# Attention and expert layer on one core: transposes gathered into longer runs, and one round of four PSUM banks

## The chip, the core and the metric

The kernel runs on one core of one Trainium2 chip. The metric is the device time of one execution in microseconds (us), the median of several runs. The engines are TensorE (PE in the profile: matmuls, and weight loads as PEld), VectorE (DVE), ScalarE (ACT), GpSimd (POOL) and SyncE (SP), which issues most of the DMAs. Every engine takes its own instructions in order; engines wait for each other through semaphores. PE writes into PSUM, which has eight banks of 128 x 512 words; DVE and ACT read them out.

## What is computed

Causal attention with a decay, and behind it a layer of eight experts of which each token takes one. Cut to what matters:

```python
# q, k, v: (8, 8, 576, 64); f: (8, 8, 576)
cum = np.cumsum(np.log(np.clip(f, 0.0001, 1.0)), axis=-1)
scores = q @ k^T / sqrt(64) + cum[..., :, None] - cum[..., None, :]
scores = where(causal mask, -1e9, scores); scores -= max over the row
attn = exp(scores); attn /= sum over the row + 1e-9
x = (attn @ v) as (4608 tokens, 512)
# experts: logits = x @ w_gate; e = argmax; gate = softmax's share of e
out = gate * (relu(x @ w1[e]) @ w2[e])
```

## The kernel before

**Pairs and steps.** The attention stage goes over 32 pairs of heads (four pairs to each of the 8 batches), numbered n. A pair's 2 x 576 rows are cut into tiles: (j, t) is head j's tile t of 128 rows, t = 0 to 3, and the last 64 rows of both heads make one joint tile. A row tile t meets only t+1 column tiles, since the mask cuts off the rest. The main loop (L732 to L815) gives each pair seven steps i = 0 to 6. Steps 0 and 1 compute the scores of (0,3) and (1,3), 512 columns each; step 2 those of (0,2) and (0,0) in one bank; step 3 (1,2) and (1,0); step 4 (0,1) and (1,1); step 5 the joint tile in two halves of 288 columns, in two banks.

**What is done with a score tile.** PE computes it (`smm`, L414) into a bank of the pool `ps_s`, which has three banks and goes round. DVE adds the mask, takes the row's extreme and writes the result to SBUF (`s_red`, L421; a short record behind it reads the accumulator). ACT takes the exponential in place (`s_exp`, L428). One pair later PE turns (transposes) the tile in blocks of 128 x 128 (`turn`, L477) into a bank, and ACT and DVE copy the bank to the array aT (`copy_on`: L473 on ACT, L471 on DVE). Step i of pair n holds the turns of pair n-1's tile of the same step: `t_steps(n - 1)[i]`. The larger tile of a bank is copied by ACT, the small ones (0,0) and (1,0) by DVE out of the same bank, and the tiles of step 4 by DVE. The joint tile's last 68 columns are turned right behind its second half, in that half's bank (`t_last`). Two pairs later, in step 1, PE multiplies with v (`av`, L553) and ACT copies out (L561).

**Between them, every fourth pair a batch is finished.** `fin_tasks` puts tasks into steps of the four pairs that follow: turning the batch's result back into rows of tokens (`fin_x`: four turns, then DVE's scaling into a row tile, L599, and a DMA to x_dram), the gate's logits (`fin_logits`), and the routing's small steps on DVE. The four pairs of such a group are told apart below as first to fourth: n = 6, 10, 14, ... are first. DVE also rounds the next pair's k (`k_first`, L373), and POOL prepares the rest of its operands.

**Order.** The engines' queues follow the order in which the loop writes the work: a step's scores and their DVE reductions, then tasks in `among`, then the step's turns with their copies, then the step's exponentials on ACT, then, in step 1, the products with v, then the step's `tasks`. Nothing is reordered afterwards (`InOrder.pin`).

**Banks.** Three for scores, two for turns (`ps_t`), one each for the two products with v and the tasks in alternation (`ps_v`, `ps_m`), and one fixed for routing.

## Time and profile before

| what | value |
|---|---|
| median of three runs (792.42 to 795.17) | 792.57 us |
| the profiled execution's own time | 791.58 us |
| its span | 789.8 us |
| PE busy, share of the span | 768.5 us, 97% |
| DVE, ACT, POOL busy | 587.0, 511.2, 543.8 us |
| granted TensorE clock, mean | 0.999 |
| DVE waits of L471 for ACT's L473 | 2.9 us in 8 waits |

The attention stage fills about the first 331 us of the span, the experts the rest. A row of the profile has the engine, the source line, the operation, what it writes and reads by the program's names, and the shape; the timeline's rows begin with the start and the duration in us, and a bracket tells what idle time came before and what ended it. `x4` is the number of instructions that a row merges.

### The profile page before, as it was taken

The numbers are of one execution on the slowest core, as the hardware profiler recorded it, in microseconds if no ns is written. First come the engines' busy times: TensorE is split into PE (matmuls) and PEld (weight loads), VectorE is DVE, ScalarE is ACT, GpSimd is POOL, SyncE is SP. The second block draws the span as 40 slices with busy tenths as digits, with TensorE's granted clock in tenths as the row PEclk, the third lists the DMA queues.
The fourth block names the chain that finished last, engine by engine and source line by source line (L and its number), as shares of the span: only waits on it lengthen the run. The fifth ranks groups of instructions, "written<-read, shape, count | busy, mean of one in ns | idle before, by whom it ended". The sixth has DMA issues, their size and how long they took to land.

```text
span 789.8 us, 16191 instructions
## 1 busy us (share of the span) xinstructions
PE 768.5 (97%) x5496; PEld 672.3 (85%) x5496; DVE 587.0 (74%) x1654; ACT 511.2 (65%) x1278; POOL 543.8 (69%) x466
## 2 busy tenths in 40 slices
PE   4999999999999999999999999999999999999996
PEld 3888888888888888888999899898898998998985
DVE  6688989898989899755589848578497487485630
ACT  6798888888888888944466546366366465463621
POOL 6999898989898989753487647556565575475311
PEclk9999999999999999999999999999999999999999
DMA  7998877787787874533445362353433433523200
GB/s 182 224 208 188 198 182 189 188 185 183 180 200 174 203 173 120 178 114 118 124 134 160 107 198 83 103 189 93 143 105 107 156 93 107 181 70 110 98 28 32
DMA packets 66825, 114.70 MB, mean 145 GB/s; under 512 B 8295, under 2 KB 39015, under 8 KB 63412
## 3 DMA queue, kind: packets, MB, share of 16 engines
q1 hardware_dynamic: 59700, 93.71, 45.8%
q0 software_dynamic: 6400, 19.93, 7.8%
q8 instruction: 44, 0.72, 0.4%
q14 instruction: 41, 0.34, 0.1%
q10 hardware_dynamic: 640, 0.01, 0.0%
HBM read 94.05 MB, written 20.55 MB: 145 GB/s over the span
## 4 chain that ended last, share of the span: by engine, by line
PE 89%; DVE 6%; ACT 2%; POOL 1%; SPq 1%; issue 1%; DMA 1%; POOLq 0%; DVEq 0%; ACTq 0%
PE ps L1200 29%; PE ps L1400 19%; PE ps L414 14%; PE ps L553 10%; PE ps L477 9%; PE ps L1170 4%; PE pr L1400 1%; DVE sc L421 1%; PE ps L1356 1%; DVE qk L373 1%; ACT sc L428 1%; DVE aT L471 1%; SPq L217 1%; ACT aT L473 1%; PE pr L993 1%
## 5 line engine op out<-in xcount | busy, mean ns | idle before, releaser
L428 ACT ACTIVATE sc<-sc,nmx 128x512 f32<-128x512 f32 (+3 forms) x256 | 142.3, 558 | 7.3 <-DVE nmx L421 5.5
L414 PE MATMUL ps<-qk 128*128 128x288 f32 (+4 forms) x384 | 124.9, 356 | 10.7 <-ACT qk L355 10.4
L421 DVE CUSTOM_DVE_ANT_0 sc<-ps,mask 128x512 f32<-128x512 f32 (+3 forms) x256 | 115.1, 483 | 16.4 <-PE ps L414 15.1
L1200 PE MATMUL ps<-w_0w,hhw 128*128 128x512 f32 x280 | 112.9, 403 | 0.0
L1400 PE MATMUL ps<-X_0w,w1s 128*128 128x320 f32 x504 | 111.7, 309 | 0.0
L1200 PE MATMUL ps<-w_0w,hl 128*128 128x512 f32 x280 | 110.8, 396 | 0.0
L1200 PE MATMUL ps<-w_1w,hhw 128*128 128x512 f32 x280 | 110.4, 394 | 0.0
L414 PE MATMUL ps<-k,q 68*128 68x288 f32 (+4 forms) x384 | 107.2, 327 | 1.5 <-DMA q<-xT0w 1.5
L1208 POOL DMA_INDIRECT out<-y,si_fast x37 | 37.3, 1009 | 96.6 <-ACT y L1207 87.6
L473 ACT COPY aT<-ps 128x512 f32<-128x512 f32 (+1 forms) x156 | 82.8, 531 | 20.4 <-PE ps L477 20.2
L553 PE MATMUL ps<-aT,va_t 128*64 128x256 f32 (+3 forms) x896 | 94.6, 354 | 0.0
L330 POOL TENSOR_TENSOR k<-raw,qk 64x1152 fp32r<-64x1152 f32 x30 | 79.8, 2659 | 18.4 <-DVE qk L373 18.4
L330 POOL TENSOR_TENSOR qk<-raw,qk 64x1280 fp32r<-64x1280 f32 x30 | 88.1, 2936 | 2.4
L1400 PEld LDWEIGHTS ps<-X_0w,w1s 128*128 128x128 f32 x504 | 84.3, 188 | 0.0
L414 PEld LDWEIGHTS ps<-qk 128*128 128x128 f32 x384 | 71.1, 197 | 14.1 <-ACT qk L355 10.4
L1207 ACT ACTIVATE y<-ps,g_fast 128x512 f32<-128x512 f32 x37 | 25.5, 690 | 87.0 <-PE ps L1200 64.9
L553 PEld LDWEIGHTS ps<-aT,va_t 128*64 128x64 f32 x896 | 58.9, 137 | 26.0 <-issue 0.7
L1400 PE MATMUL ps<-X_1w,w1s 128*128 128x320 f32 x252 | 77.9, 309 | 0.0
L414 PEld LDWEIGHTS ps<-k,q 68*128 68x128 f32 x384 | 72.7, 199 | 3.0 <-issue 2.6
L1447 POOL TENSOR_TENSOR u<-u,u 128x320 f32<-128x320 f32 x27 | 23.7, 878 | 60.6 <-DVE u L1445 60.3
L1200 PEld LDWEIGHTS ps<-w_0w,hl 128*128 128x128 f32 x280 | 52.5, 187 | 12.8
L1200 PEld LDWEIGHTS ps<-w_1w,hhw 128*128 128x128 f32 x280 | 52.8, 189 | 11.0
(242 smaller groups left out, 1900.6 us busy)
## 6 DMA issues: line engine op xcount, KB each, us to landing
raw<-in_qkT SPq DMA_DIRECT2D x52, 608.0 KB
w1r<-in_w SPq DMA_DIRECT2D x112, 128.0 KB
w<-in_w SPq DMA_DIRECT2D x28, 512.0 KB
va_t<-in_va SPq DMA_DIRECT2D x32, 256.0 KB
x_dram<-row SPq DMA_DIRECT2D x32, 256.0 KB
raw<-in_qkT SPq DMA_DIRECT2D x12, 320.0 KB
wraw<-in_w SPq DMA_DIRECT2D x7, 512.0 KB
raw<-in_qkT SPq DMA_DIRECT2D x12, 288.0 KB
```

What stands on the lines that cost most here:

```text
L330: return eng.tensor_tensor(o, raws[n][p0 : p0 + 64, c0:c1], ops[n][0][p0 : p0 + 64, c0:c1].bitcast(F32), ALU.subtract,)
L414: note(nc.tensor.matmul(out, ql[:, q0 : q0 + P], kl[:, j, k0 : k0 + kw], start=(i == 0), stop=(i == last),))
L421: V.tensor_tensor_reduce(dst[:, 0 : src.shape[1]], src, m, -0.125, init, ALU.add, ALU.min, nms[n][:, col : col + 1],)
L428: nc.scalar.activation(x, x, AF.Exp, bias=nms[n][:, col : col + 1], scale=-1.0, accum_out=acc)
L473: nc.scalar.copy(dst, src)
L477: note(nc.tensor.transpose(out.bitcast(F32R), words, c.identr))
L553: c.last_av = note(nc.tensor.matmul(pv[j * HD : (j + 1) * HD, q0 - qa : qb - qa], l, r, start=(blk == 0), stop=(blk == nb - 1),))
L1170: c.note(nc.tensor.matmul(ph[:, 0:n], w[:, wi, fs], x[xi][:, kt, :], start=(k == 0), stop=(k == 3 * KT - 1),))
L1200: c.note(nc.tensor.matmul(py, rows(hi_, ft), w[wi], start=(ft + k == 0), stop=(ft == FT - 1 and k == 2),))
L1207: nc.scalar.activation(y, py, AF.Copy, scale=g[:, s : s + 1])
L1208: nc.gpsimd.indirect_dma_start(out=self.out, out_offset=bass.IndirectOffsetOnAxis(ap=si[:, s : s + 1], axis=0), in_=y, in_offset=None, bou ...
L1400: self.nc.tensor.matmul(bank[:, 0:HN], w[:, wi, mat, kt], x[xi][:, kt, :], start=start and k == 0, stop=k == 5, skip_group_check=True,)
```

## The change

Three things. The first turns of a pair, those of tile (0,3), move from step 0 of the next pair to the end of step 5 of their own, behind the last turns of the pair before. The turns of the third and fourth tiles, (0,2) with (0,0) and (1,2) with (1,0), stand together in step 3. And the turns, the products with v, the row tasks and the logits all take their bank from one round of four (`ps_t`, `ps_t`, `ps_v`, `ps_m`). Some tasks move by a step or to the front of a step's turns (`~1` means among, ahead of the turns of step 1).

```diff
         def t_tiles(n, items, engs):
             aT = aTs[n]
-            pt = psum(ps_t)
+            pt = next_bank()
...
+        banks = itertools.cycle((ps_t, ps_t, ps_v, ps_m))
+        next_bank = lambda: psum(next(banks))
         lasts = {}
...
-            for (qa, qb, nb), bank in zip(AV, (ps_v, ps_m)):
-                pv = psum(bank)
+            for qa, qb, nb in AV:
+                pv = next_bank()
...
-            r = [(0, 3, lg[0]), (1, 0, lambda: fin_logits(b, 1, ps_m)), (1, 1, softmax),
-                 (1, 1, expert), (2, 1, gate)]
+            r = [(0, 4, lg[0]), (1, ~1, lg[1]), (1, 1, softmax), (1, 1, expert), (2, 1, gate)]
...
-                r += [(0, 2, fx[0]), (0, 4, fx[1]), (2, 2, fx[2]), (2, 3, fx[3]), (3, 1, slot),
+                r += [(0, 3, fx[0]), (0, 5, fx[1]), (2, 3, fx[2]), (2, 4, fx[3]), (3, 1, slot),
                       (3 + late, 1, lo), (3, 2, hi), (4, late, table)]
-                r += [(4, 0, lambda: fin_x(b, 4, bank=ps_m)) if late else (3, 3, fx[4])]
+                r += [(4, ~1, fx[4]) if late else (3, 3, fx[4])]
...
+        turns = {1: (1,), 3: (2, 3), 4: (4,), 5: (5,)}
...
             ts_ = t_steps(n - 1) if 0 < n <= NP else []
+            if ts_:
+                ts_[0] = None
...
-                if ts_ and ts_[i]:
-                    step(ts_[i])
+                for k in (turns if n < NP else {i: (i,)}).get(i, ()) if ts_ else ():
+                    if ts_[k]:
+                        step(ts_[k])
+                if i == 5 and n < NP:
+                    step(t_steps(n)[0])
```

What this does to the queues, in pair n = 12, a third of its group. On ACT, before, from the copy of the turns of (0,2) to the copy of the joint turns (`aT_97` is the array of the pair before, `sc_02_59` the scores of (0,2)):

```order
L473 COPY aT_97<-ps 128x3x128
L428 ACTIVATE sc_02_59,ssum<-sc_02_59,nmx 128x384
L428 ACTIVATE sc_02_59,ssum<-sc_02_59,nmx 128x128
L473 COPY aT_97<-ps 128x3x128
L428 ACTIVATE sc_12_65,ssum<-sc_12_65,nmx 128x384
L428 ACTIVATE sc_12_65,ssum<-sc_12_65,nmx 128x128
```

and now:

```order
L429 ACTIVATE sc_02_59,ssum<-sc_02_59,nmx 128x384
L429 ACTIVATE sc_02_59,ssum<-sc_02_59,nmx 128x128
L474 COPY aT_97<-ps 128x3x128 x2
L429 ACTIVATE sc_12_65,ssum<-sc_12_65,nmx 128x384
L429 ACTIVATE sc_12_65,ssum<-sc_12_65,nmx 128x128
```

The first copy has moved behind the two exponentials of (0,2) and (0,0). On DVE, in the same pair, before, from the reduction of (0,0) to that of (1,1) (`128x128` copies are the small tiles, L599 the rows of a finished batch):

```order
L421 ISA sc_02_59,nmx<-ps,mask 128x128
L421 ISA nmx 128x1
L471 COPY aT_97<-ps 128x128
L599 TENSOR_TENSOR row<-ps,rinv 128x512
L421 ISA sc_12_65,nmx<-ps,mask 128x384
L421 ISA nmx 128x1
L421 ISA sc_12_65,nmx<-ps,mask 128x128
L421 ISA nmx 128x1
L471 COPY aT_97<-ps 128x128
L599 TENSOR_TENSOR row<-ps,rinv 128x512
L421 ISA sc_01_61,nmx<-ps,mask 128x256
```

and now, on to the joint tile's first half:

```order
L422 ISA sc_12_65,nmx<-ps,mask 128x128
L422 ISA nmx 128x1
L472 COPY aT_97<-ps 128x128 x2
L603 TENSOR_TENSOR row<-ps,rinv 128x512
L422 ISA sc_01_61,nmx<-ps,mask 128x256
L422 ISA nmx 128x1
L422 ISA sc_11_67,nmx<-ps,mask 128x256
L422 ISA nmx 128x1
L472 COPY aT_97<-ps 128x2x2x128
L603 TENSOR_TENSOR row<-ps,rinv 128x512
L422 ISA sc_J,nmx<-ps,mask 128x288
```

The two small copies stand together behind all four reductions, and the second row stands behind the copy of (0,1) and (1,1). On PE, before, from the joint tile's turns to the products with v, at the end of pair 13 (`qk_1453` and `k_0_207` are the next pair's operands, `xT1w` a row's turns):

```order
L477 MATMUL ps<-identr,sc_Jw 128x128 x4
L414 MATMUL ps<-qk_1453 128x512
L414 MATMUL ps<-k_0_207,q_0_205 128x512
L477 MATMUL ps<-identr,sc_03w 128x128 x4
L477 MATMUL ps<-identr,xT1w 64x128 x4
L414 MATMUL ps<-qk_1453 128x512
L414 MATMUL ps<-k_0_207,q_0_205 128x512
L477 MATMUL ps<-identr,sc_13w 128x128 x4
```

and now:

```order
L478 MATMUL ps<-identr,sc_Jw 128x128 x4
L478 MATMUL ps<-identr,sc_03w 128x128 x4
L415 MATMUL ps<-qk_1452 128x512
L415 MATMUL ps<-k_0_207,q_0_205 128x512
L415 MATMUL ps<-qk_1452 128x512
L415 MATMUL ps<-k_0_207,q_0_205 128x512
L478 MATMUL ps<-identr,xT1w 64x128 x4
L478 MATMUL ps<-identr,sc_13w 128x128 x4
```

The turns of (0,3) follow the joint turns, the two large score tiles follow each other, and the row's turns stand behind both.

## The prediction

> **What bounds the kernel now.** I read the page first, then the stage table, then the instructions of PE, DVE and ACT in time, for two pairs of heads in the steady part. The page's first engine row and its row on the chain that ended last:

> ```profile
> PE 768.5 (97%) x5496; PEld 672.3 (85%) x5496; DVE 587.0 (74%) x1654; ACT 511.2 (65%) x1278; POOL 543.8 (69%) x466
> PE 89%; DVE 6%; ACT 2%; POOL 1%; SPq 1%; issue 1%; DMA 1%; POOLq 0%; DVEq 0%; ACTq 0%
> ```

> TensorE has nearly no empty time and carries the chain. A busy PE record says little about waits, though, since records overlap; what counts is the distance from start to start. The change touches only the attention stage, and there the table of stages (PE, PEld, DVE, ACT, POOL busy, clock, DMA) shows four engines close together:

> ```profile
> 100.00:140.00 40.00, 39.59 (x378) 33.81 (x376) 36.53 (x144) 33.87 (x104) 35.77 (x24) 1.00 0.78 187
> ```

> DVE is busy 91% here, so its own order can pace PE. I call the scores of tiles (0,2) and (0,0) s02, of (1,2) and (1,0) s12, of (0,1) and (1,1) s01, of the joint tile's halves J0 and J1, of (0,3) and (1,3) s03 and s13, and their turns t02 and so on. One pair's PE starts, pair n=12, the third of a group of four; s03 and s13 at its end belong to the next pair, t03 and t13 to this one:

> ```profile
> 133.07 0.44 PE L414 MATMUL ps<-qk 128*128 128x384 f32 x1
> ...
> 133.70 0.51 PE L477 MATMUL ps<-identr,sc_02w 128*128 128x128 f32 x4
> ...
> 134.38 0.41 PE L414 MATMUL ps<-qk 128*128 128x384 f32 x1
> ...
> 134.98 0.50 PE L477 MATMUL ps<-identr,sc_12w 128*128 128x128 f32 x4
> ...
> 135.66 0.35 PE L414 MATMUL ps<-qk 128*128 128x256 f32 x1
> ...
> 136.51 0.50 PE L414 MATMUL ps<-qk 128*128 128x288 f32 x2
> ...
> 137.64 0.54 PE L477 MATMUL ps<-identr,sc_Jw 128*68 128x128 f32 x5
> 138.02 0.46 PE L414 MATMUL ps<-qk 128*128 128x512 f32 x1
> ...
> 138.56 0.46 PE L477 MATMUL ps<-identr,sc_03w 128*128 128x128 f32 x4
> 138.85 0.49 PE L414 MATMUL ps<-qk 128*128 128x512 f32 x1
> 139.18 0.39 PE L414 MATMUL ps<-k,q 68*128 68x512 f32 x1
> 139.41 0.46 PE L477 MATMUL ps<-identr,sc_13w 128*128 128x128 f32 x4
> ```

> The same pair on DVE, from the reduction of s02 to that of J0 (the record after it reads its accumulator):

> ```profile
> 133.90 0.56 DVE L421 CUSTOM_DVE_ANT_0 sc<-ps,mask 128x384 f32<-128x384 f32 x1
> ...
> 134.38 0.29 DVE L421 CUSTOM_DVE_ANT_0 sc<-ps,mask 128x128 f32<-128x128 f32 x1
> ...
> 134.76 0.29 DVE L471 COPY aT<-ps 128x128 f32<-128x128 f32 x1
> 134.97 0.68 DVE L599 TENSOR_TENSOR row<-ps,rinv 128x512 f32<-128x512 f32 x1
> 135.56 0.55 DVE L421 CUSTOM_DVE_ANT_0 sc<-ps,mask 128x384 f32<-128x384 f32 x1
> ...
> 136.04 0.28 DVE L421 CUSTOM_DVE_ANT_0 sc<-ps,mask 128x128 f32<-128x128 f32 x1
> ...
> 136.25 0.28 DVE L471 COPY aT<-ps 128x128 f32<-128x128 f32 x1
> ...
> 137.05 0.41 DVE L421 CUSTOM_DVE_ANT_0 sc<-ps,mask 128x256 f32<-128x256 f32 x1
> ...
> 137.73 0.68 DVE L471 COPY aT<-ps 128x512 f32<-128x512 f32 x1
> 138.34 0.45 DVE L421 CUSTOM_DVE_ANT_0 sc_J<-ps,mask 128x288 f32<-128x288 f32 x1
> 138.71 0.08 DVE L421 DVE_READ_ACCUMULATOR2_ANT nmx<- 128x1 f32 x1
> ```

> And on ACT, where copies of turns alternate with exponentials:

> ```profile
> 134.25 0.48 ACT L473 COPY aT<-ps 128x384 f32<-128x384 f32 x1 [0.46 <-PE ps L477]
> 134.63 0.61 ACT L428 ACTIVATE sc<-sc,nmx 128x384 f32<-128x384 f32 x1
> ...
> 135.23 0.39 ACT L428 ACTIVATE sc<-sc,nmx 128x128 f32<-128x128 f32 x1
> ...
> 135.62 0.47 ACT L473 COPY aT<-ps 128x384 f32<-128x384 f32 x1
> 136.16 0.62 ACT L428 ACTIVATE sc<-sc,nmx 128x384 f32<-128x384 f32 x1
> ```

> Two couplings are to be seen. First, DVE's copy of (0,0) starts at 134.76, 0.03 after ACT's copy out of the same bank ends (134.25 + 0.48): DVE waits for ACT. Second, s13 takes the bank of J0, as the pool of three banks goes round, and starts at 138.85, 0.06 after J0's accumulator is read (138.71 + 0.08). In the pair before it stands just so, DVE's read ahead of PE's s13:

> ```profile
> 129.10 0.09 DVE L421 DVE_READ_ACCUMULATOR2_ANT nmx<- 128x1 f32 x1
> ```
> ```profile
> 129.24 0.50 PE L414 MATMUL ps<-qk 128*128 128x512 f32 x1
> ```

> So in these pairs PE is at the end of a DVE chain: what comes to DVE ahead of J0 comes to PE.

> **The change part by part.** *Turns in longer runs, on PE.* After turns the first matmul of 512 columns takes 0.33 (138.85 to 139.18) and the next, behind another score, 0.23 (139.18 to 139.41). With s13 right behind s03 it takes 0.46 in place of 0.56: 0.10 saved. Eight turns take 0.68 (133.70 to 134.38, four of them a row's), 0.085 each, so t03 behind the joint turns costs 0.34 in place of 0.29 (138.56 to 138.85): 0.05 lost. For s12 right behind s02 I take nothing: s02 ends in a matmul of 128 columns, behind which weights are late either way; bounds are plus and minus the same 0.10. PE alone thus gains 0.05 a pair. Worked for this pair: s02 0.63, s12 0.60, twelve turns 1.02, s01 with its turns 0.85, a row's turns 0.34, J0 and J1 1.13, their turns 0.38, t03 0.34, s03 0.54; the sum is 5.83, and s13 could start at 138.90.

> *The order on ACT and DVE.* The copies of t02 and t12 now stand in ACT's queue behind the exponentials of (0,2) and (0,0), and DVE's two small copies stand together, ahead of s01's reductions. DVE's queue is in order, so behind its wait for ACT stand the row, s01, the copy of t01 and J0. In the pair of the rows: DVE reduces s02 at 133.90 as now, then (0,0) at 134.38, s12 at 134.59 (0.21 on, as from 136.04 to 136.25) and 135.07 (0.48 on), and is free at 135.28. s12 is there in time: PE starts it at 133.70, and s02 took 0.83 from PE's start to DVE's (133.07 to 133.90), so 134.53. ACT's exponential follows a reduction's start by 0.60 (135.56 to 136.16): 134.50. The next comes 0.60 later (134.63 to 135.23), the copy 0.39 after that (135.23 to 135.62), at 135.49, and takes 0.48: 135.97. DVE's first copy starts at 136.00, so DVE has stood for 0.72. ACT's second copy starts 0.38 after the first (134.25 to 134.63) and takes 0.47: 136.34; DVE's second copy is at 136.37, 0.16 more waiting. The row follows 0.21 later (134.76 to 134.97) at 136.58, and takes 0.59 to 0.60; s01 at 137.18, the copy of t01 0.68 on (137.05 to 137.73) at 137.86, the second row 0.61 on (137.73 to 138.34) at 138.47, J0 at 139.06. Now it is at 138.34: **0.72 later**. J0's read ends 0.45 on, s13 starts at 139.57 instead of the 138.90 that PE could do, and the 0.10 that s13 saved is lost again, as its first weights are late.

> *The fourth pair*, n=13, has one routing step on DVE in that stretch and no row; DVE's rows, then PE's last turns of a row and s13:

> ```profile
> 143.50 0.56 DVE L421 CUSTOM_DVE_ANT_0 sc<-ps,mask 128x384 f32<-128x384 f32 x1 [0.63 <-PE ps L414]
> ...
> 145.91 0.41 DVE L421 CUSTOM_DVE_ANT_0 sc<-ps,mask 128x256 f32<-128x256 f32 x1
> ...
> 147.20 0.45 DVE L421 CUSTOM_DVE_ANT_0 sc_J<-ps,mask 128x288 f32<-128x288 f32 x1
> ```
> ```profile
> 147.76 0.41 PE L477 MATMUL ps<-identr,xT0w 128*64 128x128 f32 x4
> 148.01 0.45 PE L414 MATMUL ps<-qk 128*128 128x512 f32 x1
> ```

> By the same steps DVE's first copy is at 143.50 + 0.60 + 0.60 + 0.39 + 0.48 + 0.03 = 145.60, the second at 145.97, s01 at 146.18: 0.27 later than 145.91, with J0 as much. PE's s13 can then start 0.45 and 0.06 after J0's 147.47, at 147.98, no later than now. But the row's four turns that stand ahead of s13 now (0.25, from 147.76 to 148.01) come behind it, so t13 starts about 0.25 later; and the routing matmuls right behind this pair wait for DVE too, which is 0.27 late. I take 0.27; bounds 0 and 0.27.

> *First and second pairs.* In the first, the second row (fx1) moves from ahead of J0 to behind it: 0.72 less 0.60, so 0.12. The second pair begins on DVE with that 0.60 in arrears; its rank steps stand ahead of the two copies and fill most of the wait, between 0 and 0.72 of it; I take 0.10 more, so 0.70.

> *One round of four banks.* The turns' waits for a bank become older: a bank comes again after four uses instead of two. These waits are small already, and where they go J0's read is next, so I count nothing; bounds 0 and 0.1 a pair gained. The products with v take banks that ACT emptied half a pair earlier: nothing, hidden behind the scores. *SP* issues the rows' writes a step later, and their consumers are batches away; POOL's order stays as it was. Nothing for either.

> **The sum.** A group of four pairs: 0.12 + 0.70 + 0.72 + 0.27 = 1.81. Six groups lie whole in the steady part (n=6 to 29): 10.9. The other pairs with scores on both sides, seven, lie between -0.05 and +0.27 each; at 0.15 that is 1.1. In all 12.0 on the profiled execution's 791.58 (span 789.8): 803.6. The stage behind attention is PE's throughout, so nothing there takes it back. The median of the runs shown, 792.57, lies 1.0 above that execution; I forecast 804.5 for it.

> **The rivals.** *PE's saving arrives (not slower).* If DVE's copies were not held behind ACT's exponentials, DVE would gain on PE and only the 0.05 a pair and up to 0.1 for bank waits would count: about 30 pairs, 1.5 to 4.5 less, so 790 (788 to 791). It decides from where J0's read ends before PE can do s13: in the third pair a DVE wait under 0.1 in place of 0.88. For it speaks that PE's waits are small now and the page gives DVE only 6% of the chain; against it, the 0.03 and 0.06 of the rows above, and that the order of both queues is fixed.

> *Only the third pair pays.* If the first pairs' arrears vanish in DVE's idle 0.63 of the row at 143.50, 6 times 0.72 remain: 4.3 less some PE saving, 796.

> *A slow cast.* DVE's cast of k is short or long by what POOL does:

> ```profile
> 131.44 0.77 DVE L373 CAST qk<-raw 128x1152 fp32r<-128x1152 f32 x1
> ...
> 150.52 2.06 DVE L373 CAST qk<-raw 128x1152 fp32r<-128x1152 f32 x1
> ```

> Were one more cast of a group long, 6 times 1.29 would be 7.7 more: 812; two, 820. [...]

> That the instructions don't move as said is excluded by the built order.

> **How the numbers follow.** Forecast 0.64, its own range 798 to 809: the second pair's bounds move it by -3.6 or +3.7, the fourth pair's and the single pairs' by -2.5 or +1. PE's saving 0.20, only the third pair 0.08, slow cast 0.08. 0.5% of 792.57 is 4.0, about what a measurement of this kernel can tell from no change. Faster by more: a third of the second case, 0.07. Within it: the rest of it and part of the third, 0.16. Slower: 0.77. For 8 in 10 I go from 790.5, which leaves out about half of the saving case, to 813, which leaves out two slow casts: together some 0.14.

> **What would show it.** Right: waits of DVE copies for ACT copies (L471 behind L473) of 15 to 25 us in all, DVE idle some 0.7 ahead of the first small copy in first and third pairs, s13 starting 0.05 to 0.06 after J0's read in nearly every pair, and third pairs 0.7 longer from s02 to t13. Wrong: DVE's copies starting with no wait, or s13 at 0.46 behind s03 with the read long done. If the third pair's J0 comes less than 0.3 later on DVE, the working is wrong at its first step; if it comes 0.7 later and s13 does not, the bank is not the one that I named.

## The result and the profile after

The changed kernel takes 801.94 us (median of five runs, 800.90 to 803.32) against 792.57 for the one before (five runs, 792.17 to 795.17). The ratio, taken over all runs and so not the quotient of the two medians, is 1.0109, with a 95% interval of 1.0089 to 1.0130. The forecast was 804.5, its range 798 to 809. The profiled execution has a span of 800.2 instead of 789.8, so 10.4 more, where the sum had 12.0. Of these 10.4, 10.0 lie in the attention stage (the last but one products with v begin at 341.15 instead of 331.12), and 0.4 behind it.

The page's first engine row and the row of the chain that ended last:

```profile
PE 772.5 (97%) x5496; PEld 670.0 (84%) x5496; DVE 588.1 (73%) x1654; ACT 510.0 (64%) x1278; POOL 543.3 (68%) x466
PE 70%; DVE 17%; DMA 4%; ACT 3%; issue 2%; POOL 2%; SPq 0%; ACTq 0%; DVEq 0%; POOLq 0%
```

PE's busy share hardly tells anything (97% before and after), but its share of the chain has fallen from 89% to 70%, and DVE's has gone from 6% to 17%. The same stretch of the stage table as before:

```profile
100.00:140.00 40.00, 38.94 (x363) 32.52 (x364) 34.37 (x140) 32.26 (x98) 34.29 (x24) 1.00 0.79 181
```

All engines do less in the same 40 us, at the same clock: nobody got busier, they wait for each other. The waits (total us, times, longest) name the two couplings that the prediction had named:

```profile
DVE aT L472 <- ACT aT L474: 14.3, 24, 0.9
PEld ps L415 <- DVE nmx L422: 14.3, 28, 0.7
```

The first was 2.9 in 8 waits before (the prediction named 15 to 25), the second 0.4 in one wait. The second total is no measure of the loss: a kernel below has 8.6 of it (changed, turns apart, rows back) and takes no longer than the kernel before. Now pair n=12, the third of its group, on PE: the scores of (0,2), the next pair's s03 and s13, and t13:

```profile
135.49 0.44 PE L415 MATMUL ps<-qk 128*128 128x384 f32 x1
...
140.99 0.47 PE L415 MATMUL ps<-qk 128*128 128x512 f32 x1
...
142.00 0.50 PE L415 MATMUL ps<-qk 128*128 128x512 f32 x1 [0.31 <-DVE nmx L422]
...
142.56 0.46 PE L478 MATMUL ps<-identr,sc_13w 128*128 128x128 f32 x4
```

On DVE, from the reduction of s02 to the read of J0's accumulator:

```profile
136.33 0.56 DVE L422 CUSTOM_DVE_ANT_0 sc<-ps,mask 128x384 f32<-128x384 f32 x1
...
137.50 0.29 DVE L422 CUSTOM_DVE_ANT_0 sc<-ps,mask 128x128 f32<-128x128 f32 x1
...
138.42 0.67 DVE L472 COPY aT<-ps 128x128 f32<-128x128 f32 x2 [0.63 <-ACT aT L474]
139.00 0.68 DVE L603 TENSOR_TENSOR row<-ps,rinv 128x512 f32<-128x512 f32 x1
139.60 0.41 DVE L422 CUSTOM_DVE_ANT_0 sc<-ps,mask 128x256 f32<-128x256 f32 x1
...
140.29 0.69 DVE L472 COPY aT<-ps 128x512 f32<-128x512 f32 x1
140.89 0.68 DVE L603 TENSOR_TENSOR row<-ps,rinv 128x512 f32<-128x512 f32 x1
141.49 0.45 DVE L422 CUSTOM_DVE_ANT_0 sc_J<-ps,mask 128x288 f32<-128x288 f32 x1
141.86 0.08 DVE L422 DVE_READ_ACCUMULATOR2_ANT nmx<- 128x1 f32 x1
```

And on ACT, where the two copies (merged into one row) come behind both exponentials:

```profile
136.93 0.62 ACT L429 ACTIVATE sc<-sc,nmx 128x384 f32<-128x384 f32 x1 [0.89 <-DVE nmx L422]
...
137.54 0.39 ACT L429 ACTIVATE sc<-sc,nmx 128x128 f32<-128x128 f32 x1
...
137.93 0.83 ACT L474 COPY aT<-ps 128x384 f32<-128x384 f32 x2
138.66 0.62 ACT L429 ACTIVATE sc<-sc,nmx 128x384 f32<-128x384 f32 x1
```

Counted from PE's start of s02 (133.07 before, 135.49 now), the small copy begins at 2.93, J0 at 6.00 and s13 at 6.51; the forecast's steps gave 2.93, 5.99 and 6.50, and before it was 1.69, 5.27 and 5.78. s13 starts 0.06 after the read ends (141.94). From s02 to t13 the pair takes 7.07 instead of 6.34. So the working holds to a hundredth here; whether it also names the right cause is another question, which the experiments answer.

To compare kernels, the table below gives the distance from one pair's first product with v to the next pair's, for the group n = 10 to 13, in us, from one profiled execution each. Times are medians; each ratio is taken over all runs, against runs of the kernel before on the same chip, whose medians lay between 791.8 and 792.6. In the changed kernel these are the first and the last:

```profile
110.68 1.84 PE L557 MATMUL ps<-aT,va_t 128*64 128x256 f32 x16
...
152.36 0.44 PE L557 MATMUL ps<-aT,va_t 128*64 128x256 f32 x2
```

| kernel | first | second | third | fourth | group | time | ratio to before, interval |
|---|---|---|---|---|---|---|---|
| before | 12.18 | 9.27 | 9.60 | 9.12 | 40.17 | 792.57 | 1 |
| changed | 11.94 | 10.00 | 10.34 | 9.40 | 41.68 | 801.94 | 1.0109 (1.0089 to 1.0130) |
| round of four alone | 12.20 | 9.27 | 9.61 | 9.11 | 40.19 | 794.50 | 1.0028 (1.0016 to 1.0041) |
| first turns alone | 11.71 | 9.70 | 10.03 | 9.60 | 41.04 | 799.20 | 1.0090 (1.0075 to 1.0105) |
| long run alone | 11.86 | 10.13 | 9.80 | 10.01 | 41.80 | 805.73 | 1.0163 (1.0150 to 1.0176) |
| rows later alone | 14.41 | 9.18 | 10.07 | 9.10 | 42.76 | 813.45 | 1.0262 (1.0237 to 1.0286) |
| changed, turns apart, rows back | 12.29 | 9.19 | 9.62 | 9.12 | 40.22 | 792.18 | 1.0004 (0.9994 to 1.0014) |
| changed, rows back | 11.95 | 9.41 | 9.73 | 9.40 | 40.49 | 794.91 | 1.0032 (1.0020 to 1.0045) |
| changed, turns apart | 12.12 | 9.78 | 10.06 | 9.15 | 41.11 | 797.73 | 1.0084 (1.0067 to 1.0102) |
| changed, exponentials held | 11.63 | 9.54 | 9.68 | 9.11 | 39.96 | 791.21 | 0.9991 (0.9982 to 1.0001) |
| the same, rows back | 11.80 | 9.20 | 9.55 | 9.11 | 39.66 | 789.14 | 0.9959 (0.9946 to 0.9973) |
| changed, four banks for scores | 12.69 | 9.09 | 10.49 | 9.12 | 41.39 | 800.46 | 1.0105 (1.0090 to 1.0119) |

### The profile page after: what moved, and what is told of

Its sections match the earlier page's. It is cut to its first block, busy times and chain, and to the rows that moved or that the text cites. A ratio compares the mean times of both kernels' runs of the same rounds, so it can differ in the third digit from the quotient of the medians.

```text
span 800.2 us, 16208 instructions
## 1 busy us (share of the span) xinstructions
PE 772.5 (97%) x5496; PEld 670.0 (84%) x5496; DVE 588.1 (73%) x1654; ACT 510.0 (64%) x1278; POOL 543.3 (68%) x466
## 4 chain that ended last, share of the span: by engine, by line
PE 70%; DVE 17%; DMA 4%; ACT 3%; issue 2%; POOL 2%; SPq 0%; ACTq 0%; DVEq 0%; POOLq 0%
PE ps L1210 28%; PE ps L1410 18%; PE ps L415 7%; DVE sc L422 6%; PE ps L557 6%; PE ps L1180 4%; PE ps L478 3%; DMA va_t<-in_va 3%; DVE aT L472 2%; ACT aT L474 2%; DVE row L603 2%; DVE sc_J L422 1%; DVE qk L374 1%; PE pr L1410 1%; ACT sc L429 1%
## 5 line engine op out<-in xcount | busy, mean ns | idle before, releaser
L415 PE MATMUL ps<-qk 128*128 128x288 f32 (+4 forms) x384 | 122.7, 354 | 13.6 <-ACT qk L356 10.2
L422 DVE CUSTOM_DVE_ANT_0 sc<-ps,mask 128x512 f32<-128x512 f32 (+3 forms) x256 | 112.5, 484 | 13.2 <-PE ps L415 11.8
L331 POOL TENSOR_TENSOR qk<-raw,qk 64x1280 fp32r<-64x1280 f32 x30 | 88.1, 2936 | 2.4
L474 ACT COPY aT<-ps 128x512 f32<-128x512 f32 (+1 forms) x156 | 76.8, 532 | 1.4 <-PE ps L478 1.4
L472 DVE COPY aT<-ps 128x128 f32<-128x128 f32 (+2 forms) x132 | 51.8, 395 | 16.8 <-ACT aT L474 14.3
```

The lines of the kernel that those rows point to most:

```text
L331: return eng.tensor_tensor(o, raws[n][p0 : p0 + 64, c0:c1], ops[n][0][p0 : p0 + 64, c0:c1].bitcast(F32), ALU.subtract,)
L415: note(nc.tensor.matmul(out, ql[:, q0 : q0 + P], kl[:, j, k0 : k0 + kw], start=(i == 0), stop=(i == last),))
L422: V.tensor_tensor_reduce(dst[:, 0 : src.shape[1]], src, m, -0.125, init, ALU.add, ALU.min, nms[n][:, col : col + 1],)
L472: V.tensor_copy(dst, src)
L474: nc.scalar.copy(dst, src)
```

## The experiments

The first theory was the prediction's: DVE's two small copies wait for ACT's copies out of the same banks, which the merge put behind two exponentials (**order**). Its rivals: turns that wait for banks of the new round (**banks**), and the rows moved by a step, which load DVE at another place (**rows**).

**Turns apart.**

```diff
-        turns = {1: (1,), 3: (2, 3), 4: (4,), 5: (5,)}
+        turns = {1: (1,), 2: (2,), 3: (3,), 4: (4,), 5: (5,)}
```

> The changed kernel, but the turns of the third tile stand in step 2 and those of the fourth in step 3 again. Order theory (DVE's small copies wait for ACT's copies, which stand behind two exponentials): waits of DVE copies for ACT copies fall from 14.3 us to under 4; second and third pairs lose their 0.73 each, fourth pairs keep 0.15 to 0.29 because the row's turns still stand behind the second score of 512 columns; 801.9 less 8.8 (six groups) less about 1 in the single pairs gives 792, range 790 to 794. Bank theory (the round of four makes turns wait for banks that are emptied late) and row theory (the rows that moved by a step load DVE ahead of the joint tile): both stay, so 799 or more.

It took 797.73, not 792: undoing the merge gives back less than half. DVE still waits 7.8 us for ACT, and its third pair looks so:

```profile
135.06 0.56 DVE L422 CUSTOM_DVE_ANT_0 sc<-ps,mask 128x384 f32<-128x384 f32 x1
...
137.27 0.29 DVE L472 COPY aT<-ps 128x128 f32<-128x128 f32 x1 [0.38 <-ACT aT L474]
...
139.96 0.45 DVE L422 CUSTOM_DVE_ANT_0 sc_J<-ps,mask 128x288 f32<-128x288 f32 x1
```

From s02 to J0 DVE takes 4.90: 5.16 in the changed kernel, 4.44 before. The copies stand in ACT's queue as before the change, and yet DVE waits 0.38 at the second small copy. What is missing is the row: in the kernel before, a row of 0.60 stood on DVE ahead of s12's reductions (134.97 to 135.56), and when DVE came to that copy at 136.25, ACT's copy, which began at 135.62, was over. So the order theory in its pure form fell, and a third one came: the row was the **cover** of a wait that had always been there.

**Exponentials held.** The long run stays, but ACT does its two copies first:

```diff
+                if i == 2 and n < NP:
+                    held = e_
+                elif i == 3 and n < NP:
+                    held()
+                    e_()
-                if e_:
+                elif e_:
                     e_()
```

> The changed kernel with the one run of turns kept, but ACT does the exponentials of step 2 behind its two copies of step 3. Order theory: the copies start as soon as PE has turned the tiles, DVE waits under 0.2 per pair, 790 to 795; what is left above the first experiment is the exponentials' delay of 0.8 on ACT, which nobody waits for until the next pair's turns. If instead the long run itself costs (PE turns both tiles before DVE and ACT get either), or banks or rows, it stays at 799 or more.

791.21, within the range, and with an interval that holds 1: no different from the kernel before. Third pair, ACT and DVE (4.49 from s02, at 133.31, to J0, at 137.80):

```profile
134.22 0.86 ACT L474 COPY aT<-ps 128x384 f32<-128x384 f32 x2 [0.96 <-PE ps L478]
```
```profile
134.74 0.67 DVE L472 COPY aT<-ps 128x128 f32<-128x128 f32 x2
```

ACT now waits for PE's turns, and DVE's first copy starts 0.05 later than the 0.21 that a step from a reduction takes; no wait of these copies for ACT is long enough to be listed. In sum the whole loss goes, with banks and rows as in the change; of the pairs, only the second keeps 0.27. ACT's copies standing behind exponentials are therefore needed for the third pair's loss; the moved rows alone don't make it.

**Rows back.** The rows in their old steps, with the turns merged, and with the turns apart:

```diff
-                r += [(0, 3, fx[0]), (0, 5, fx[1]), (2, 3, fx[2]), (2, 4, fx[3]), (3, 1, slot),
+                r += [(0, 2, fx[0]), (0, 4, fx[1]), (2, 2, fx[2]), (2, 3, fx[3]), (3, 1, slot),
```

> The changed kernel with the four rows (fx0 to fx3) in the steps that they had before; the long run of turns stays. Cover theory (a row of 0.60 stood on DVE between the reductions of two steps and filled its wait for ACT's copies; the change took this cover away and, by the merge, made the wait longer): in the third pair DVE's wait falls from 0.71 to 0.1 to 0.3 in all, second and third pairs lose 0.3 to 0.5 each, 801.9 less 6 x 0.9 gives 796.5, range 795 to 799. Pure order theory (the merge alone): the row just moves within a fixed wait, third pairs by less than 0.15, 800 to 802.

> The kernel of the first experiment (third and fourth tiles' turns apart, 797.7) with the rows in their old steps too; first turns moved and the round of four stay. Cover theory: DVE's third pair runs as in the kernel before (5.27 from PE's start of the third tile to DVE's start of the joint tile, 5.73 in the first experiment), 797.7 less 6 x (0.5 + 0.4) gives 792, range 790.5 to 793. Rival, that first turns or the round of four carry what was left there: 796 to 798.

794.91, just under the range of the cover theory, and 792.18, within its range. In the first of them, DVE:

```profile
136.64 0.56 DVE L422 CUSTOM_DVE_ANT_0 sc<-ps,mask 128x384 f32<-128x384 f32 x1
...
137.33 0.69 DVE L603 TENSOR_TENSOR row<-ps,rinv 128x512 f32<-128x512 f32 x1
...
138.73 0.67 DVE L472 COPY aT<-ps 128x128 f32<-128x128 f32 x2
...
141.20 0.45 DVE L422 CUSTOM_DVE_ANT_0 sc_J<-ps,mask 128x288 f32<-128x288 f32 x1
```

The row is back between the reductions of s02 and s12; the first copy follows the last reduction (138.41 and 0.21) with 0.11 of waiting in place of 0.71, and s02 to J0 takes 4.56. With these two kernels the four combinations are there: the later rows cost 0.0080 of the time with the turns apart and 0.0077 with the long run, the long run costs 0.0028 with the old rows and 0.0025 with the later ones. Within their intervals the two add up, and the rows are three quarters of them. The pairs tell the rows' part in two. In the third pair they cost 0.44 with the turns apart and 0.61 with the long run: this is the cover. In the second they cost 0.59 both times, and this is no cover, but the second row, which now stands behind the joint tile, so that DVE still has to do it when that pair begins. First turns and the round of four, with the logits and the fifth row moved, cost nothing together (1.0004).

**Exponentials held and rows back.** Both edits together:

> The second experiment (long run kept, ACT's copies ahead of the held exponentials, 791.2) with the rows in their old steps. Cover theory: DVE waits for ACT no more there, so a cover is worth nothing; but fx1 stands ahead of the joint tile again in the first pair and leaves no arrears for the second pair, whose 9.54 could fall to 9.25: 791.2 less 6 x 0.3 gives 789.5, range 788 to 791.5. If the later steps were what made the first pair shorter (12.2 to 11.63), that comes back: 791 to 794.

789.14, in the range: the ratio is 0.9959 with an interval below 1, so this version beats both kernels. It keeps the whole change but the steps of four rows, and has two exponentials held back. DVE begins s02 at 133.83 and

```profile
138.10 0.45 DVE L422 CUSTOM_DVE_ANT_0 sc_J<-ps,mask 128x288 f32<-128x288 f32 x1
```

is 4.27 later, less than before. The second pair's arrears go as expected (9.54 to 9.20).

**Four banks for scores**, three for the rest, to take s13 off J0's bank:

```diff
-        banks = itertools.cycle((ps_t, ps_t, ps_v, ps_m))
+        banks = itertools.cycle((ps_t, ps_t, ps_m))
...
+        s_banks = itertools.cycle((ps_s, ps_s, ps_s, ps_v))
+        s_bank = lambda: psum(next(s_banks))
-            pb = psum(ps_s)
+            pb = s_bank()
```

> The changed kernel with four banks in the scores' round and three in the round for turns, products and rows. DVE's waits for ACT stay (about 14 us), but the second score of 512 columns no longer takes the joint tile's bank. Order theory with that bank as the coupling: PE's waits for nmx there go, third pairs 0.5 to 0.7 shorter (DVE is idle 0.95 ahead of the next pair and takes up its delay), second pairs too except for rank's wait of about 0.6; 801.9 less 6 x (0.6 + 0.1 + 0.2) gives 796.5, range 793 to 799. If the lateness of DVE reaches PE some other way (the joint halves or the turns wait in its place): 800 to 803. Bank theory: fewer banks for turns make it worse, above 803.

800.46: outside the 793 to 799 of the order theory, and in the 800 to 803 of a lateness that reaches PE some other way. In all that is hardly anything, and yet the pairs differ. Second pairs fall from 10.00 to 9.09, more than hoped for, and s13 waits no more (s03 and s13 take 1.00 together in every pair, 1.57 in the changed kernel's third). But third and first pairs get longer, since the turns of (0,1), in a round of three, now meet the bank that DVE's small copy holds:

```profile
138.89 0.37 PE L481 MATMUL ps<-identr,sc_01w 128*128 128x128 f32 x2 [0.67 <-DVE aT L475]
```

So J0's bank is the place at which DVE's lateness reaches PE in third pairs, as said; opened with a bank from the turns, the same lateness comes through the turns.

**Parts alone on the kernel before.** The long run alone (turns of both tiles in step 3), the first turns alone, and the round of four alone:

```diff
-                if ts_ and ts_[i]:
-                    step(ts_[i])
+                for k in ({2: (), 3: (2, 3)} if n < NP else {}).get(i, (i,)) if ts_ else ():
+                    if ts_[k]:
+                        step(ts_[k])
```

> The kernel before with only the turns of the third and fourth tiles put together in step 3. Order theory: all of the loss is here; DVE waits for ACT's copies 12 to 16 us, second and third pairs 0.5 to 0.73 longer, 797 to 803. Bank theory or row theory: none of the cause is here, 792 to 794.

```diff
+            if ts_:
+                ts_[0] = None
...
                 if ts_ and ts_[i]:
                     step(ts_[i])
+                if i == 5 and n < NP:
+                    step(t_steps(n)[0])
```

> The kernel before with only the first turns of a pair moved to the end of its predecessor's turns. By the prediction's sum PE saves 0.05 a pair where DVE does not hold it: 0 to 1.5 less, 791 to 792.5. If moving those turns is itself a cause of the loss (the second score of 512 columns now stands right behind the first and reaches the joint tile's bank 0.3 sooner, and gains nothing there): 792 to 793, with as many PE waits for nmx more as PE saved. If ACT's copy of those turns ahead of the joint exponential hurts: 794 or more.

```diff
-            pt = psum(ps_t)
+            pt = next_bank()
...
-                pv = psum(bank)
+                pv = next_bank()
...
-            px = psum(ps_s if (b, t) == (B - 2, 0) or b == B - 1 and t > 1
-                      else bank or fin_bank[0])
+            px = (psum(ps_s) if (b, t) == (B - 2, 0) or b == B - 1 and t > 1
+                  else fin_bank[0]())
```

> The kernel before with the one round of four banks alone; turns, rows and tasks stay. The prediction counted nothing for it, with up to 0.1 a pair gained at most: 789.5 to 793. If the products with v, now in the same round as turns that ACT and DVE empty late, wait for banks: 793.5 or more.

805.73, 799.20 and 794.50. All three miss their first ranges, on the bad side; the third lies where products with v that wait for banks would put it, but the pairs show no such wait. The first two show what the round of four is for. With two banks for turns, the run of t02 and t12 fills both, and t01 must wait for DVE's copies of (0,0) and (1,0); and t03, moved up behind the joint turns, needs the bank that DVE is still copying t01 from. From the waits of the first (PE's weight loads of turns, for DVE's copies; 3.2 in 16 waits before), and from PE in the second:

```profile
PEld ps L477 <- DVE aT L471: 18.7, 30, 1.0
```
```profile
141.57 0.53 PE L477 MATMUL ps<-identr,sc_03w 128*128 128x128 f32 x4 [0.29 <-DVE aT L471]
```

The round alone leaves every pair of the steady part as it was. Its 3.0 us of longer span are 0.5 in attention and 2.5 behind the issue of the last store, where the trace shows no work; what those 2.5 are stays open.

**Rows later alone** on the kernel before, the same edit the other way round:

> The kernel before with only the four rows (fx0 to fx3) a step later. Cover theory: the row no longer stands between the two small copies on DVE, which then waits 0.3 to 0.4 for ACT's second copy, and the second row stands ahead of the joint tile with one step less between: third pairs 0.3 to 0.5 longer, second pairs 0.2 to 0.5 by arrears, 792.3 plus 6 x 0.7 gives 796.5, range 794 to 799. If the cover matters only once the turns stand in one run: 792 to 793.5.

813.45, far above. The third pair is 0.47 longer, as the cover theory has it, with DVE's waits for ACT at 8.0 us instead of 2.9. But second pairs are 0.09 shorter, and first pairs 2.2 to 4.5 longer, by a wait that has nothing to do with cover: tasks alternate between two banks there by the step's number, and a moved row meets the bank of the logits, once in each of the six first pairs (1.6):

```profile
PE ps L477 <- DVE gq L641: 9.8, 6, 1.6
```

Two of the first pairs are 2.2 longer, the other four 3.0 to 4.5. The mean granted clock of this execution besides is 0.985, where that of the kernel before is 0.999; the 0.014 between them is by estimate at most 11.4 us of the span of 812.4, and where in the span it lies was not shown. For the cover theory only the third pair counts here; the total says nothing.

**POOL's subtraction in parts.** First pairs are 0.24 to 0.29 shorter after the change in four of the six groups, against the forecast (0.24 and 0.45 longer in those from n=6 and n=18), since PE's wait for the routing operand (L986 before, L996 now) is gone: 16 gate matmuls and that wait took 1.59, now 1.11. Ahead of that operand stands DVE's cast in DVE's queue. POOL's subtraction and the cast, in the kernel before:

```profile
108.89 2.91 POOL L330 TENSOR_TENSOR qk<-raw,qk 64x1280 fp32r<-64x1280 f32 x1
```
```profile
110.35 2.07 DVE L373 CAST qk<-raw 128x1152 fp32r<-128x1152 f32 x1
```

In the changed kernel, the same place and the group from n=18, whose first pair is longer (12.67 instead of 12.21):

```profile
110.16 2.93 POOL L331 TENSOR_TENSOR qk<-raw,qk 64x1280 fp32r<-64x1280 f32 x1
...
194.41 2.91 POOL L331 TENSOR_TENSOR qk<-raw,qk 64x1280 fp32r<-64x1280 f32 x1
```
```profile
112.25 1.45 DVE L374 CAST qk<-raw 128x1152 fp32r<-128x1152 f32 x1
...
195.61 2.32 DVE L374 CAST qk<-raw 128x1152 fp32r<-128x1152 f32 x1
```

Each time the cast ends 0.61 or 0.62 after the subtraction (111.80 and 112.42; 113.09 and 113.70; 197.32 and 197.93), whenever it began. POOL's subtraction ends 2.41 behind the first product with v in place of 3.05 (111.80 less 108.75; 113.09 less 110.68), and the cast ends sooner with it. That a group now takes PE longer, with POOL's work as before, would explain the 2.41, but was not tested, and why POOL is late in the group from n=18 is open. To test that the cast waits for the one POOL instruction, the subtraction in four instructions of 320 columns, on the kernel before and on the fastest version:

```diff
-            lo(nc.gpsimd, n, qk1[64:128, 0:QW], 64, 0, QW)
+            for c0 in range(0, QW, QW // 4):
+                lo(nc.gpsimd, n, qk1[64:128, c0 : c0 + QW // 4], 64, c0, c0 + QW // 4)
```

> The kernel before with POOL's subtraction for q (2.91 in one instruction, L330) cut into four of 320 columns, some 0.75 each. If DVE's cast of k stands for as long as the POOL instruction that runs when it is issued (in three places it ended 0.60 to 0.62 behind the end of one): the cast of first pairs falls from 2.06 to 0.8 to 1.4, PE's wait of 0.48 ahead of the routing matmuls in first pairs goes, 792.3 less 6 x 0.48 gives 789.4, range 788.5 to 790.5. If DVE is slow whenever POOL works at all, whatever the length of its instructions: cast stays at 1.9 to 2.1 and the time at 792 to 793.

> The fastest version so far (long run kept, exponentials held, rows in their old steps, 789.1) with POOL's subtraction for q in four parts. If the cast waits for one POOL instruction only: PE's wait ahead of the routing matmuls in first pairs (16 gate matmuls take 1.25 instead of 1.11) goes, 6 x 0.14, so 788.3, range 787 to 789. If not: 789 to 790.

797.03 (1.0056, interval 1.0037 to 1.0076) and 796.80 (1.0056, 1.0037 to 1.0075): both are slower than the kernel before, the second is 7.7 us slower than the version that it is built on, and both lie outside all their ranges, though the first pair's cast got shorter as expected. On the kernel before, it takes 0.75 instead of 2.07, with POOL's four parts drawn out around it, PE's wait goes, and the pair falls from 12.18 to 11.73. But in the four groups from n=14 on, POOL's last part meets the second pair's cast (below in n=19):

```profile
111.85 4.34 POOL L330 TENSOR_TENSOR qk<-raw,qk 64x320 fp32r<-64x320 f32 x4
...
202.33 3.36 POOL L330 TENSOR_TENSOR qk<-raw,qk 64x320 fp32r<-64x320 f32 x4
```
```profile
113.06 0.75 DVE L374 CAST qk<-raw 128x1152 fp32r<-128x1152 f32 x1
...
204.87 1.44 DVE L374 CAST qk<-raw 128x1152 fp32r<-128x1152 f32 x1
```

That cast ends at 206.31, 0.62 behind POOL's 205.69, and the second pair takes 9.94 instead of 9.27; in the group before them the cast stays at 0.76 and the second pair at 9.26. Besides, the subtraction costs POOL more in parts: 109.2 us in all instead of 88.1, which uses up its wait of 18.4 for k (1.4 is left). Of the span's 5.8 us, 1.0 arise in the six groups, 2.1 ahead of them and 2.8 in the pairs n=30 and 31. The mean granted clock of this execution is 0.994, but executions with 0.998 (796.07 to 796.74) are only some 1 us shorter than those with 0.994 (797.32 and 797.43), so the rest is open. In the fastest version second pairs go from 9.20 to 10.11; there the cast stands behind POOL's own cast of q (124.06 to 125.30) and ends 0.62 after it.

The cast of n=19 began 0.82 ahead of the end of POOL's four parts, less than one part's 0.87, and ended 0.62 behind it. In the first pair it is POOL that is drawn out, and its four parts take 4.34 instead of 3.36, though by the recorded starts it was POOL that came first:

```profile
112.68 1.86 POOL L330 TENSOR_TENSOR qk<-raw,qk 64x320 fp32r<-64x320 f32 x1
```

This second part began 0.38 ahead of the cast (113.06), and yet it takes 1.86 instead of 0.87 while the cast takes its 0.75. So the recorded starts don't tell which of the two is drawn out, and no row shows what decides it.

## Why the prediction was right, and where it was wrong

**The sum.** By group, forecast and measured (n = 10 to 13): first pair +0.12 and -0.24, second +0.70 and +0.73, third +0.72 and +0.74, fourth +0.27 and +0.28; together 1.81 and 1.51. Over all six groups 10.9 was forecast and 9.8 measured (the distance from n=6 to n=30 went from 240.92 to 250.76); the six first pairs, -0.35 together where 0.7 was forecast, account for the difference. The other pairs were to give 1.1 and give 0.2: what n=2 to 5 lose, the start had gained. Behind attention 0 was said and 0.4 came.

**The first pair is the term that was mis-sized.** "In the first, the second row (fx1) moves from ahead of J0 to behind it: 0.72 less 0.60, so 0.12" left out that PE stands in that pair for the routing operand, and took the slow cast ahead of it at the length that it had. The slow cast stood among the rivals, "short or long by what POOL does", and the runs bear that out: in the first pairs it ends 0.61 or 0.62 behind POOL's subtraction, before the change and after. The sign was the other one: the change made the cast shorter, 1.45 for 2.07, in most groups, and longer, 2.32, in one. Without the 0.48 of that wait the pair is 0.24 longer, twice the 0.12, and by another path: s13 waits in no first pair (it starts 0.53 to 0.55 behind s03), but the logits' turns do, for the bank of DVE's small copies:

```profile
118.42 0.40 PEld L478 LDWEIGHTS ps<-identr,gT0w 128*128 128x128 f32 x4 [0.24 <-DVE aT L472]
```

**The second pair: the row's arrears, by a path not named.** That this pair begins with 0.60 in arrears on DVE is borne out: with the rows back it takes 9.41 instead of 10.00. But the larger part reaches PE ahead of J0, at the matmuls of the rank steps, whose operand DVE now has ready late:

```profile
127.28 0.18 PE L945 MATMUL pr<-ohb,trib 128*128 128x48 bf16 x1 [0.42 <-DVE ohb L929]
```

From the last scores of s12 to these matmuls PE takes 0.57 longer than before, and from s03 to t13 about 0.3 (without t03); 0.14 is saved elsewhere. The prediction had the rank steps only as work that fills DVE's wait, so the 0.73 for 0.70 is partly luck.

**The third pair: right number, half the cause.** The wait, its length, what stood behind it, J0's read and s13 came out to 0.02. But the prediction put it all on the copies behind the exponentials and gave the rows a part only in the first pair and as arrears in the second. It had placed the row rightly in DVE's queue, which is why the number was right, and had not asked what the row had been covering. Shown: ACT's late copies are needed for the loss (held exponentials take it away), and the row that no longer covers it is 0.44 to 0.61 of its 0.72 (9.62 to 10.34 in the table), depending on which of the two is undone first.

**The fourth pair** came as worked out. On DVE:

```profile
146.65 0.56 DVE L422 CUSTOM_DVE_ANT_0 sc<-ps,mask 128x384 f32<-128x384 f32 x1 [0.95 <-PE ps L415]
...
148.74 0.67 DVE L472 COPY aT<-ps 128x128 f32<-128x128 f32 x2 [0.35 <-ACT aT L474]
...
150.62 0.45 DVE L422 CUSTOM_DVE_ANT_0 sc_J<-ps,mask 128x288 f32<-128x288 f32 x1
```

DVE waits 0.35 for ACT and reaches J0 3.97 behind the reduction of s02 instead of 3.70: 0.27 late. On PE the row's four turns now stand behind s13 and move t13 by 0.24 (151.70 to 151.94):

```profile
151.70 0.41 PE L478 MATMUL ps<-identr,xT0w 128*64 128x128 f32 x4
151.94 0.48 PE L478 MATMUL ps<-identr,sc_13w 128*128 128x128 f32 x4
```

**PE's saving** of 0.05 a pair exists where DVE leaves it alone: in the fastest version t03, s03 and s13 take 1.34 in the third pair, 1.39 before. In the changed kernel it was lost to J0's read, as said: the weight load of s13 starts with its matmul at 142.00, and that one takes 0.33. For s12 right behind s02 nothing was taken, and its first matmul takes 0.23 there (136.12 to 136.35) and 0.25 behind turns (134.38 to 134.63); its weight load starts 0.05 and 0.03 ahead of it, while the one behind the 384 columns of s02 starts 0.17 ahead (135.60 and 135.77).

**The round of four at nothing** is right for itself, but it was not weighed what it carries: without it the long run costs 13.6 and the first turns 6.9.

## What to carry to other kernels

When an instruction is moved within an in-order queue, ask not only what it will delay at its new place but which wait it was filling at its old one: in the third pair here a cover of 0.60 us was worth 0.44 to 0.61, more than the 0.11 to 0.28 of the longer run of turns. A loss at one wait has two remedies, to bring its releaser forward or to put work in front of it, and here both together gave a version faster than either kernel (the rows' return then paid mostly in the second pair, 9.54 to 9.20, and less in the third, 9.68 to 9.55). And test parts of a change against each other: the long run and the first turns lost 13.6 and 6.9 us alone, for want of banks, but little (1.0032) and nothing (1.0004) together with the round.
